# Sharing the homes of softmax buffers, and keeping an o weight piece by halves, in a recurrent attention with a gated FFN

## The chip, the cores and the metric

The kernel runs on one core of a Trainium2 chip. The metric is the device time of one execution in microseconds. A profile is one further execution; its span is counted from the first to the last instruction.

## The reference

A sequence of 2048 tokens with 1024 channels goes through two branches. Branch A is a recurrence over 64 segments of 32 tokens, with 32 heads of 128. Branch B is a feed-forward net of width 3584. A gate mixes the two.

```python
x = A_x
g = _sigmoid((x * gate_w).sum(-1, keepdims=True))
for s in range(n_seg):                       # branch A
    xs = x[:, s * seg_len:(s + 1) * seg_len, :].copy()
    h = jnp.concatenate([mem, xs], axis=1)   # 8 memory rows and 32 tokens
    q = jnp.einsum('btd,dhe->bhte', h, Wq)   # k and v in the same way
    ...
    scores = jnp.where(mask[None, None], scores, -1000000000.0)
    p = _softmax(scores, axis=-1)
    o = jnp.einsum('bhqk,bhke->bhqe', p, v)
    o = jnp.einsum('bhte,hed->btd', o, Wo)
    mem = o[:, :M, :].copy()                 # the next segment's memory
    outs.append(o[:, M:, :])
b = _gelu(x @ w_gate) * (x @ w_up) @ w_down  # branch B
return g * a + (1 - g) * b
```

All tensors are bf16. Each segment needs the memory rows that the segment before it has put out, so the 64 steps are a chain.

## The kernel before

**Stages.** Up to about 145 us the kernel transposes x, computes the gate and four of the 28 columns of the net's first layer, and loads the first attention weights. From there to about 1643 us it runs the 64 steps. Then comes branch B with the mix. An operation is recorded with `op(engine, function, rd=, wr=)`; a small planner turns reads and writes of 64-byte cells of SBUF, and of PSUM banks, into semaphore waits. Each engine runs its operations in program order. Two tiles at one address are therefore kept apart by waits alone.

**Weights.** Wq, Wk, Wv and Wo are 64 pieces of 128 x 2048 bf16, 512 KB each: letter, half u of the heads (0 or 1), number 0 to 7. They are more than SBUF holds beside the rest, which is room for 52 slots. In 40 slots one piece stays for good. In 12 a pair lives by turns: (k, 0, i) and (k, 1, i) for instance share a slot, and each step loads one of the two. `PAIRS` says which:

```python
PAIRS = {"k": (0, 2, 4), "q": (), "v": (0, 1, 2, 3, 4, 6), "o": (0, 1, 2)}
```

`proj(p, s)` multiplies with the piece at place p of the walk, then calls `spent(k)`, which has SyncE load the other piece of the pair into the slot (`fetch`, line 379). Odd steps take the halves in the other order, so that the piece loaded last is used first, without another load.

**One step.** `walk` gives 64 places: k and q of the first half by turns (16), v of the first half (8), k and q of the second half (16), then o of the first half and v of the second half interleaved, then o of the second half (8). Within the first half of a letter the paired pieces come first; within the second half they come last. A projection piece of q, k or v is four matmuls of 128x512 on four column groups of the array (lines 801 and 784); a piece of o is eight of 128x256 (line 812), four for each of its two heads.

**Fills.** The last 8 rows of each segment's tokens do not depend on the memory. Their q, k, v for four segments at once are computed by `fill` (line 831) and their output rows by `wo` (line 850), eight groups of matmuls each. They lie in between: three groups of `fa` ahead of the first attention, and in this version the other five behind the last v piece.

**Work hung into a step.** `on(letter, half, n, f)` puts work ahead of a place of the walk. In this order:
- `rest_k` (line 896) copies k of the last 8 tokens to columns 32 to 39 of kT, on POOL. It is called for the first head half early in a step, and for the second half after the first scores.
- `turn` transposes k and q and writes kT (ACT) and qT (DVE).
- `scores` (lines 713 to 727) writes a PSUM bank; it also has POOL clear pB.
- `softmax` (lines 730 to 743): exp to E8 on ACT; on DVE the sum, the reciprocal, the product pA, its transpose tA, the product pB, its transpose tB.
- `attend` (line 755) and `attend_tail` (line 767) multiply with tA and tB, then copy oT to SBUF on ACT and DVE, then oRc on POOL (line 778).

At the end of a step ACT writes a_bf (line 677), eight small transposing matmuls (line 1022) make the memory columns of the next hT, and the next step begins.

**DMA queues.** SyncE issues all weight loads, and those of qkr, hT and vB; ACT issues the stores; POOL issues oR and hR.

**Homes.** tA, E8, pA, pB each have a home of their own here; a_bf shares pA's, tB shares E8's.

Of the kernel before, what the change touches and what calls it, by code (L numbers as in the profile page):

```python
# [8 lines left out]
ALU = mybir.AluOpType  # L9
# [186 lines left out]
def bass_gated_mix__memory_aug_recurrent_mem_tr__geglu_ffn__prompt_kernel(  # L196
# [35 lines left out]
    with ExitStack() as es:  # L232
# [55 lines left out]
        oRc = al("oRc", [128, 2, NB, 16])  # L288
        vB = al("vB", [128, 2, 128])
        kT = al("kT", [128, 4, 4, LQ])  # L290
        tA = al("tA", [128, 8, 32])
        E8 = al("E8", [128, 8, LQ])
        oT = al("oT", [128, 4, 4, OW])
        tok = al("tok", [128, 512])
        stage = al("stg", [128, 512])
        pA = al("pA", [128, 8, 32])
        pB = al("pB", [128, 288])
        a_bf = al("a_bf", [128, 256], at=pA.off)
        vAs = [al("vA0", [128, 4, 128], at=oT.off), al("vA1", [128, 4, 128], at=tok.off)]
        qT = al("qT", [128, 4, 4, 32], at=stage.off)  # L300
        tok2 = al("tok2", [128, 512], at=oT.off + 1024)
        tB = al("tB", [128, 8, 32], at=E8.off)

        PIECE = 4096
        cur[0] = (cur[0] + 63) // 64 * 64
# [9 lines left out]
        NSLOT = NLOW + (top - cur[0]) // PIECE  # L315


        PAIRS = {"k": (0, 2, 4), "q": (), "v": (0, 1, 2, 3, 4, 6), "o": (0, 1, 2)}

        def seq(m, r):  # L320
            pairs = PAIRS[m] if m in "vo" else sorted({*PAIRS["k"], *PAIRS["q"]})
# [44 lines left out]
        def dst(t, k):  # L366
            return t[:, :].rearrange("p (h f) -> p h f", h=2) if k[0] == "o" else t[:, :]

        nlane = [0]
        done = [0] * len(hosts)  # L370

        def fetch(n):
            k, t = uses[n][done[n]], slots[n]
            if paired(k):
                lane = f"sl{n}"
            else:
                lane = f"res{nlane[0] % 8}"
                nlane[0] += 1
            op("sp", lambda e: e.dma_start(dst(t, k), src(k)), wr=[t.r()], lane=lane)  # L379

        def first(k):
            n = home[k]
            if done[n] == 0 and uses[n][0] == k:
                fetch(n)

        def spent(k):
# [41 lines left out]
        wgp = [al(f"wgp{h}", [128, KC, NJP * 64]) for h in range(2)]  # L428
        wup = [al(f"wup{h}", [128, KC, NJP * 64]) for h in range(2)]
        gpre = [al(f"gpre{i}", [128, NJP, FB]) for i in range(2)]  # L430
        memT = al("memT", [128, 64])
        xr1 = cur[0]
        cur[0] += 2 * TB * KC * 4 * NB
        assert cur[0] <= top
        cur[0] = low
        tp = [al(f"tp{t}", [128, FB], FP32) for t in range(2)]
        s1 = al("s1", [128, FB], FP32)
        xr = [al(f"xr{i}", [128, TB, KC, 4, NB], at=(cur[0], xr1)[i]) for i in range(2)]
        cur[0] += xr[0].nb
        tokB = al("tokB", [128, 512], at=oT.off)  # L440
        stv = al("stv", [128, 512], at=slots[-2].off)
        st0 = [al(f"st0{i}", [128, 4, 2, 128], at=slots[-1].off + 2048 * i) for i in range(2)]
        dl = al("dl", [128, NT], FP32, at=stage.off + stage.nb - 64)
        assert cur[0] <= dl.off
        hR1 = al("hR1", [128, KC, 32], at=pB.off)
        assert hR1.nb <= pB.nb
        hT = hTs[0]

        def gelu(hg, hu, bg, bu, n, gt, gt_r):
# [279 lines left out]
        def softmax():  # L729
            op("act", lambda e: e.activation(E8[:, :, :].rearrange("p a c -> p (a c)"), PB[SS][:, 0:320], ACTF.Exp, scale=scale),  # L730
               rd=[BK(SS)], wr=[E8.r()])
            op("dve", lambda e: e.tensor_reduce(sm, E8[:, :, :], AX.X, ALU.add), rd=[E8.r()], wr=[st8.r(8, 16)])
            op("dve", lambda e: e.reciprocal(sm, sm), rd=[st8.r(8, 16)], wr=[st8.r(8, 16)])
            op("dve", lambda e: e.tensor_tensor(out=pA[:, :, :], in0=E8[:, :, 0:32], in1=b8(sm, 32), op=ALU.mult),
               rd=[E8.r(), st8.r(8, 16)], wr=[pA.r()])
            op("dve", lambda e: e.transpose(tA[:, :, :].rearrange("p a c -> p (a c)"), pA[:, :, :].rearrange("p a c -> p (a c)")),
               rd=[pA.r()], wr=[tA.r()])
            op("dve", lambda e: e.tensor_tensor(
                out=pB[:, :].rearrange("p (j a) -> p j a", j=4)[:, :, 0:64].rearrange("p j (c k) -> p j c k", c=2)[:, :, :, 0:8],
                in0=E8[:, :, 32:40].rearrange("p (j c) k -> p j c k", c=2),  # L740
                in1=sm.rearrange("p (j c) -> p j c", c=2).unsqueeze(3).to_broadcast([128, 4, 2, 8]), op=ALU.mult),
               rd=[E8.r(), st8.r(8, 16)], wr=[pB.r()])
            op("dve", lambda e: e.transpose(tB[:, :, :].rearrange("p a c -> p (a c)"), pB[:, 0:256]),
               rd=[pB.r()], wr=[tB.r()])
# [13 lines left out]
                return ins  # L758
            op("pe", f, rd=[vA.r(), tA.r()], wr=[BK(b) for b in bo])

        def attend_tail(u, r):
            bo = bos[r]

            def f(e):
                for g in range(4):
                    r = slice(32 * g, 32 * g + 32)
                    ins = e.matmul(PB[bo[g]][:, 0:4 * OW].rearrange("p (j c) -> p j c", j=4)[:, :, NR:OW], lhsT=vB[r, u, :],  # L767
                                   rhs=tB[r, :, :].rearrange("p (j a) c -> p j (a c)", a=2)[:, :, NR:OW],
                                   start=False, stop=True, skip_group_check=True)
                return ins  # L770
            op("pe", f, rd=[tB.r(), vB.r()], wr=[BK(b) for b in bo])
            n = 4 * OW
# [16 lines left out]
        def proj(p, s):  # L789
            k = at_step(p, s)  # L790
            w = slots[home[k]]
            i = k[2]
            mine = spot[walk[p][:2]]
            one, end = p == mine[0], p == mine[-1]
            if k[0] != "o":
                h, bk = hTs[s % 2], bank_of[walk[p][:2]]

                def f(e):
                    for g in range(4):
                        at = PB[bk][32 * g:32 * g + 32, :], h[:, i, :], w[:, g * 512:(g + 1) * 512]  # L800
                        ins = again(e, g, *at, one, end) if k[0] == "q" else e.matmul(*at, start=one, stop=end)  # L801
                    return ins
                op("pe", f, rd=[h.r(32 * i, 32 * i + 32), w.r()], wr=[BK(bk)])
            else:
                r = walk[p][1]
                gp_, jj = i // 2, i % 2

                def f(e):
                    for hh in range(2):
                        for g in range(4):  # L810
                            c = hh * 1024 + g * 256
                            ins = e.matmul(PB[XO][32 * g:32 * g + 32, 0:256], lhsT=oT[:, gp_, 2 * jj + hh, 0:32],  # L812
                                           rhs=w[:, c:c + 256], start=(r == 0 and one and hh == 0), stop=(r == 1 and end and hh == 1))
                    return ins
                n = 4 * OW
                op("pe", f, rd=[oT.r(gp_ * n, (gp_ + 1) * n), w.r()], wr=[BK(XO)])
            spent(k)

        def holds(k, at_end=False):
# [20 lines left out]
        def wo(u, b, t=oR, ends=(True, True), at_end=False):  # L840
            out = []
            for n, i in enumerate([i for i in range(8) if i not in PAIRS["o"]] + list(PAIRS["o"])):
                k = ("o", u, i)
                w = (xo.get(k) if at_end else None) or slots[home[k]]

                def f(e, i=i, w=w, n=n):
                    for hh in range(2):
                        for g in range(4):
                            c = hh * 1024 + g * 256
                            ins = e.matmul(PB[b][32 * g:32 * g + 32, 0:256], lhsT=t[:, :, 2 * i + hh], rhs=w[:, c:c + 256],  # L850
                                           start=(ends[0] and n == 0 and hh == 0), stop=(ends[1] and n == 7 and hh == 1))
                    return ins

                def go(f=f, k=k, w=w):
                    holds(k, at_end)
                    op("pe", f, rd=[t.r(), w.r()], wr=[BK(b)])
                out.append(go)
            return out

# [43 lines left out]
        for s in range(NSEG):  # L903
# [12 lines left out]
            def on(m, r, n, *fs):  # L916
                at.setdefault(spot["k" if m == "q" else m, r][n], []).extend(fs)
# [6 lines left out]
            def some(fs, n=99):  # L924
                return lambda: run(fs, n)
# [46 lines left out]
            on("k", 1, 0, lambda: evac(bank_of["v", 0], vAs[0]))  # L972
            on("k", 1, 0, lambda: scores(ua))
            on("k", 1, 0, softmax)
            on("k", 1, 5, lambda: rest_k(ub))
            if uw is not None:
                on("k", 1, 5, lambda: load_oR(Q, uw))

# [1 line left out]
            on("o", 0, 0, lambda: evac(bank_of["q", 1], stage))  # L980
            on("o", 0, 0, some(fa, 3))
            on("o", 0, 0, lambda: attend(ua, 0))
            on("o", 0, 0, lambda: attend_tail(ua, 0))
            on("o", 0, 0, turn)
            on("o", 0, 3, lambda: scores(ub))
            on("o", 0, 3, softmax)

            on("o", 1, 0, lambda: evac(bank_of["v", 1], vAs[1]))
            on("o", 1, 0, some(fa))
            on("o", 1, 0, lambda: attend(ub, 1))  # L990
# [202 lines left out]
```

## Time and profile before

| | |
|---|---|
| three runs, median | 2194.36 us (2189.56 to 2199.25) |
| profiled execution | 2186.54 us, span 2184.8 us |
| mean granted TensorE clock | 0.985 |
| busy share | PE 91%, DVE 43%, ACT 30%, POOL 13% |
| moved by DMA | 528.78 MB, 490.16 MB of it read from HBM |
| weight loads in the steps | 394 of v, 205 of k, 205 of o, each 512 KB |
| stretch 145 to 1642 us | DMA share 0.85, 296 GB/s |

A row of a view names the line, the engine, the operation and out<-in; "sl" stands for all weight slots, so a load of v is "sl<-in_A_Wv_dram". PE's busy time counts matmuls that are in flight, so a high share does not say that PE has no time to spare. PEld is PE's loading of weights. In the chain of waits each row is a start, a length and what was running or moving then; "issue" is time without a wait that the profile shows. A load's "DMA to landing" is counted from the start of its issue to the last byte's semaphore.

### The profile page before, as it was taken

Reading aid. Unit: us, or ns where it says so; the run is one execution under the profiler, and the core shown is the slowest. Engines: PE = TensorE matmul, PEld = TensorE weight load, DVE = VectorE, ACT = ScalarE, POOL = GpSimd, SP = SyncE. Lnnn points to the kernel's source line nnn. Section 1 sums busy time; section 2 is a strip of 40 time slices with the busy share of each in tenths; the row PEclk is TensorE's granted clock in tenths of the full one; section 3 lists DMA queues with packets and bytes.
Section 4 is the critical chain, followed back from the end, with each engine's and each line's share of the span. In section 5 each row is a group of like instructions: output and inputs, shape, how many; then the busy total and the mean of one; then the engine's idle time right before and its main releaser. Section 6 shows DMA issues by size and latency. Waiting matters only on the chain.

```text
span 2184.8 us, 77490 instructions
## 1 busy us (share of the span) xinstructions
PE 1992.8 (91%) x38220; PEld 938.7 (43%) x32556; DVE 938.7 (43%) x2056; ACT 650.0 (30%) x1330; POOL 293.0 (13%) x589
## 2 busy tenths in 40 slices
PE   7878989989999898889899999999889999999999
PEld 4334444444444444444444444444344434243343
DVE  6433443444344344344434444443444526263462
ACT  4323333333333333333333333333322213032130
POOL 7211111111111111111111111111111000000000
PEclk9999999999999999999999999999998999999999
DMA  9988888888888888888878888888889200000000
GB/s 364 353 299 275 304 310 289 291 297 307 284 318 299 281 314 308 273 285 305 296 272 287 315 293 301 303 295 279 302 298 371 102 20 30 31 30 30 25 25 20
DMA packets 259022, 528.78 MB, mean 242 GB/s; under 512 B 56048, under 2 KB 109168, under 8 KB 258696
## 3 DMA queue, kind: packets, MB, share of 16 engines
q1 hardware_dynamic: 215968, 483.15, 62.2%
q10 hardware_dynamic: 34136, 20.19, 3.3%
q0 software_dynamic: 8592, 20.49, 2.6%
q8 instruction: 278, 4.55, 0.8%
q14 instruction: 48, 0.39, 0.1%
HBM read 490.16 MB, written 33.55 MB: 240 GB/s over the span
## 4 chain that ended last, share of the span: by engine, by line
PE 63%; DMA 31%; issue 2%; ACT 1%; DVE 1%; SPq 1%; POOL 0%; ACTq 0%; POOLq 0%; DVEq 0%
DMA sl<-in_A_Wv_dram 26%; PE pb L463 16%; PE pb L801 13%; PE pb L784 10%; PE pb L812 6%; PE pb L831 5%; PE pb L1148 4%; PE pb L691 3%; PE pb L850 3%; DMA sl<-in_A_Wo_dram 2%; PE pb L1126 1%; SPq L379 1%; DMA xr_scr<-xr 1%; ACT a_bf L677 1%; PE pb L755 1%
## 5 line engine op out<-in xcount | busy, mean ns | idle before, releaser
L801 PE MATMUL pb<-sl,hT 128*32 128x512 bf16 x8192 | 708.6, 381 | 98.3 <-DMA sl<-in_A_Wv_dram 83.7
L801 PEld LDWEIGHTS pb<-sl,hT 128*32 128x32 bf16 x8192 | 220.3, 96 | 496.7 <-issue 272.1
L784 PE MATMUL pb<-sl,hT 128*32 128x512 bf16 x4096 | 399.5, 379 | 0.0
L812 PE MATMUL pb<-sl,oT 128*32 128x256 bf16 x8192 | 287.0, 277 | 28.2 <-issue 21.3
L812 PEld LDWEIGHTS pb<-sl,oT 128*32 128x32 bf16 x8192 | 210.3, 98 | 72.1 <-issue 31.4
L831 PE MATMUL pb<-sl,hR 128*32 128x512 bf16 x3072 | 218.1, 394 | 19.6 <-DMA sl<-in_A_Wv_dram 10.7
L677 ACT ACTIVATE tok<-pb 128x512 bf16<-128x512 f32 x192 | 114.9, 598 | 300.2 <-PE pb L801 271.7
L778 POOL COPY oRc<-oT 128x128 bf16<-128x128 bf16 x128 | 96.9, 757 | 738.2 <-DVE oT L680 729.2
L463 PE MATMUL pb<-xT,wg 128*128 128x512 bf16 x768 | 183.1, 382 | 2.6 <-DMA wg<-in_B_w_gate_dram 2.6
L680 DVE CAST oT<-pb 128x256 bf16<-128x256 f32 x256 | 96.8, 420 | 203.9 <-PE pb L767 203.9
L463 PE MATMUL pb<-xT,wu 128*128 128x512 bf16 x768 | 182.5, 381 | 0.0
L451 ACT ACTIVATE s<-pb 128x512 f32<-128x512 f32 x112 | 66.9, 598 | 289.6 <-PE pb L463 289.6
L1148 PE MATMUL pb<-wd,GT 128*32 128x512 bf16 x1568 | 152.4, 379 | 0.0
L784 PE MATMUL pb<-wd,GT 128*32 128x512 bf16 x1568 | 152.4, 379 | 0.0
L677 ACT ACTIVATE vA<-pb 128x512 bf16<-128x512 f32 x128 | 76.4, 597 | 226.1 <-PE pb L801 226.1
L452 DVE SCALAR_TENSOR_TENSOR tp<-s,pb 128x512 f32<-128x512 f32 x112 | 76.8, 685 | 125.6 <-ACT s L451 125.2
L831 PEld LDWEIGHTS pb<-sl,hR 128*32 128x32 bf16 x3072 | 79.3, 98 | 103.9 <-issue 28.5
L726 DVE TENSOR_REDUCE st<-pb 128x8 f32<-128x320 f32 x128 | 63.0, 492 | 125.8 <-PE pb L720 125.7
L463 PEld LDWEIGHTS pb<-xT,wg 128*128 128x128 bf16 x768 | 75.1, 98 | 95.5 <-issue 6.6
L463 PEld LDWEIGHTS pb<-xT,wu 128*128 128x128 bf16 x768 | 75.5, 98 | 91.7 <-issue 1.9
L680 DVE CAST stg<-pb 128x512 bf16<-128x512 f32 x64 | 44.3, 692 | 155.2 <-PE pb L784 155.2
L455 DVE SCALAR_TENSOR_TENSOR tp<-tp,pb 128x512 f32<-128x512 f32 x112 | 77.0, 688 | 78.9 <-ACT tp L454 77.4
(107 smaller groups left out, 2046.2 us busy)
## 6 DMA issues: line engine op xcount, KB each, us to landing
sl<-in_A_Wv_dram SPq DMA_DIRECT2D x394, 512.0 KB, 8.8
sl<-in_A_Wk_dram SPq DMA_DIRECT2D x205, 512.0 KB, 5.9
sl<-in_A_Wo_dram SPq DMA_DIRECT2D x205, 512.0 KB, 7.7
sl<-in_A_Wq_dram SPq DMA_DIRECT2D x16, 512.0 KB, 13.3
qkr<-qk_scr SPq DMA_DIRECT2D x63, 128.0 KB, 8.2
qk_scr<-fqk ACTq DMA_DIRECT2D x29, 256.0 KB, 6.0
wd<-in_B_w_down_dram SPq DMA_DIRECT2D x7, 1024.0 KB, 15.3
xq_scr<-xTp SPq DMA_DIRECT2D x4, 1024.0 KB, 17.1
```

What stands on the lines that cost most here:

```text
L451: op("act", lambda e: e.activation(s1[:, :], hg, ACTF.Square, scale=SQ), rd=[BK(bg)], wr=[s1.r()])
L452: op("dve", lambda e: e.scalar_tensor_tensor(out=t[:, :], in0=s1[:, :], scalar=1.0, in1=hg, op0=ALU.add, op1=ALU.mult), rd=[BK(bg), s1.r() ...
L455: op("dve", lambda e: e.scalar_tensor_tensor(out=t[:, :], in0=t[:, :], scalar=1.0, in1=hu, op0=ALU.add, op1=ALU.mult), rd=[BK(bu), t.r()], ...
L463: ins = e.matmul(PB[bk][:, 0:FB], lhsT=w[:, kc, cc:cc + 128], rhs=x[:, :, :, kc, :].rearrange("p t i c -> p (t i) c"), start=(kc == 0), st ...
L677: op("act", lambda e: e.activation(o, i, ACTF.Copy), rd=rd, wr=wr)
L680: op("dve", lambda e: e.tensor_copy(o, i), rd=rd, wr=wr)
L778: op("pool", lambda e: e.tensor_copy(oRc[:, u, :, :].rearrange("p c (g j) -> p g j c", g=4), diag), rd=[oT.r()], wr=[oRc.r(128 * u, 128 * ...
L784: return e.add_instruction(mybir.InstMatmult(name=nc.get_next_instruction_name(), start_tensor_calc=start, stop_tensor_calc=stop, tile_siz ...
L801: ins = again(e, g, *at, one, end) if k[0] == "q" else e.matmul(*at, start=one, stop=end)
L812: ins = e.matmul(PB[XO][32 * g:32 * g + 32, 0:256], lhsT=oT[:, gp_, 2 * jj + hh, 0:32], rhs=w[:, c:c + 256], start=(r == 0 and one and hh ...
L831: ins = e.matmul(PB[b][32 * g:32 * g + 32, :], lhsT=h[:, k[2], :], rhs=w[:, g * 512:(g + 1) * 512], start=(n == 0), stop=(n == 7))
L1148: ins = again(e, q, *a, j == 0, j == NJ - 1) if hf else e.matmul(*a, start=(j == 0), stop=(j == NJ - 1))
```

## The change

1. **Pairs.** v has five pairs instead of six (3 leaves), o has four instead of three (3 joins). Slots stay 52.
2. **The o pair 3 by halves.** Its slot keeps the first head of both pieces for good. The second head, 256 KB, lives in a new tile `oh` of 2 KB per partition; each step loads the one of the other half into it.
3. **Homes.** E8 takes the home of qT (`stage`); pB and tB take that of kT; a_bf and hR1 that of tA; pA is gone, the product is made in place in E8, and the transpose reads E8 with a stride of 40 between blocks. At the start, xr and memT get other homes.
4. **Order.** rest_k of the second half comes behind the matmuls of the first attention instead of behind the first scores. Two groups of `fa` come ahead of the last five v pieces, so three instead of five stand behind the last.

```diff
+        tA = al("tA", [128, 8, 32])
+        oh = al("oh", [128, 1024])
+        a_bf = al("a_bf", [128, 256], at=tA.off)
+        E8 = al("E8", [128, 8, LQ], at=stage.off)
+        pB = al("pB", [128, 288], at=kT.off)
...
-        tB = al("tB", [128, 8, 32], at=E8.off)
+        tB = al("tB", [128, 8, 32], at=kT.off + 640)
...
-        PAIRS = {"k": (0, 2, 4), "q": (), "v": (0, 1, 2, 3, 4, 6), "o": (0, 1, 2)}
+        PAIRS = {"k": (0, 2, 4), "q": (), "v": (0, 1, 2, 4, 6), "o": (0, 1, 2, 3)}
+        HALF = 3
...
+        halved = lambda k: k[0] == "o" and k[2] == HALF
+
+        def heads_of(k):
+            t = slots[home[k]]
+            if not halved(k):
+                return [(t, 0), (t, 1024)]
+            return [(t, 1024 * k[1]), (oh, 0)]
...
         def fetch(n):
             k, t = uses[n][done[n]], slots[n]
+            if halved(k):
+                op("sp", lambda e: e.dma_start(oh[:, :], A_Wo[16 * k[1] + 2 * HALF + 1]), wr=[oh.r()], lane="oh")
+                return
...
-            op("dve", lambda e: e.tensor_tensor(out=pA[:, :, :], in0=E8[:, :, 0:32], in1=b8(sm, 32), op=ALU.mult),
-               rd=[E8.r(), st8.r(8, 16)], wr=[pA.r()])
-            op("dve", lambda e: e.transpose(tA[:, :, :].rearrange("p a c -> p (a c)"), pA[:, :, :].rearrange("p a c -> p (a c)")),
-               rd=[pA.r()], wr=[tA.r()])
+            op("dve", lambda e: e.tensor_tensor(out=E8[:, :, 0:32], in0=E8[:, :, 0:32], in1=b8(sm, 32), op=ALU.mult),
+               rd=[E8.r(), st8.r(8, 16)], wr=[E8.r()])
+            op("dve", lambda e: e.transpose(tA[:, :, :], E8[:, :, 0:32]),
+               rd=[E8.r()], wr=[tA.r()])
...
-            on("k", 1, 5, lambda: rest_k(ub))
...
-            on("o", 0, 0, lambda: attend_tail(ua, 0))
+            on("o", 0, 0, lambda: attend_tail(ua, 0, lambda: rest_k(ub)))
...
+            on("v", 1, 3, some(fa, 2))
```

After the last step, four o pieces of half 1 are loaded anew for the last `wo` instead of three.

More of the change, by code (lines that the diff above doesn't have):

```diff
@@ L290, in bass_gated_mix__memory_aug_recurrent_mem_tr__geglu_ffn__prompt_kernel @@
         kT = al("kT", [128, 4, 4, LQ])
-        tA = al("tA", [128, 8, 32])
-        E8 = al("E8", [128, 8, LQ])
         oT = al("oT", [128, 4, 4, OW])
@@ L295, in bass_gated_mix__memory_aug_recurrent_mem_tr__geglu_ffn__prompt_kernel @@
         stage = al("stg", [128, 512])
-        pA = al("pA", [128, 8, 32])
-        pB = al("pB", [128, 288])
-        a_bf = al("a_bf", [128, 256], at=pA.off)
+        tA = al("tA", [128, 8, 32])
[3 more added lines that the diff above has]
+        pB = al("pB", [128, 288], at=kT.off)
         vAs = [al("vA0", [128, 4, 128], at=oT.off), al("vA1", [128, 4, 128], at=tok.off)]
@@ L367, in dst, with regs @@
             return t[:, :].rearrange("p (h f) -> p h f", h=2) if k[0] == "o" else t[:, :]
+        halved = lambda k: k[0] == "o" and k[2] == HALF
[4 more added lines that the diff above has]
+            return [(t, 1024 * k[1]), (oh, 0)]
+        def regs(k):
+            return [t.r(c, c + 1024) for t, c in heads_of(k)]
         nlane = [0]
@@ L383, in first @@
             if done[n] == 0 and uses[n][0] == k:
+                if halved(k):
+                    t = slots[n]
+                    op("sp", lambda e: e.dma_start(t[:, :].rearrange("p (u f) -> p u f", u=2),
+                                                   A_Wo.rearrange("(u h) p f -> h p u f", u=2)[2 * HALF]), wr=[t.r()], lane="oh2")
                 fetch(n)
@@ L430, in bass_gated_mix__memory_aug_recurrent_mem_tr__geglu_ffn__prompt_kernel @@
         gpre = [al(f"gpre{i}", [128, NJP, FB]) for i in range(2)]
-        memT = al("memT", [128, 64])
+        memT = al("memT", [128, 64], at=oh.off)
         xr1 = cur[0]
-        cur[0] += 2 * TB * KC * 4 * NB
+        cur[0] += 4 * TB * KC * 4 * NB
         assert cur[0] <= top
@@ L437, in bass_gated_mix__memory_aug_recurrent_mem_tr__geglu_ffn__prompt_kernel @@
         s1 = al("s1", [128, FB], FP32)
-        xr = [al(f"xr{i}", [128, TB, KC, 4, NB], at=(cur[0], xr1)[i]) for i in range(2)]
-        cur[0] += xr[0].nb
+        xr = [al(f"xr{i}", [128, TB, KC, 4, NB], at=xr1 + i * 2 * TB * KC * 4 * NB) for i in range(2)]
         tokB = al("tokB", [128, 512], at=oT.off)
@@ L444, in bass_gated_mix__memory_aug_recurrent_mem_tr__geglu_ffn__prompt_kernel @@
         assert cur[0] <= dl.off
-        hR1 = al("hR1", [128, KC, 32], at=pB.off)
-        assert hR1.nb <= pB.nb
+        hR1 = al("hR1", [128, KC, 32], at=tA.off)
         hT = hTs[0]
@@ L759, in attend, with attend_tail @@
             op("pe", f, rd=[vA.r(), tA.r()], wr=[BK(b) for b in bo])
-        def attend_tail(u, r):
+        def attend_tail(u, r, then=None):
             bo = bos[r]
@@ L771, in attend_tail @@
             op("pe", f, rd=[tB.r(), vB.r()], wr=[BK(b) for b in bo])
+            if then:
+                then()
             n = 4 * OW
@@ L808, in f @@
                 def f(e):
-                    for hh in range(2):
+                    for hh, (w, c0) in enumerate(heads_of(k)):
                         for g in range(4):
-                            c = hh * 1024 + g * 256
+                            c = c0 + g * 256
                             ins = e.matmul(PB[XO][32 * g:32 * g + 32, 0:256], lhsT=oT[:, gp_, 2 * jj + hh, 0:32],
@@ L815, in proj @@
                 n = 4 * OW
-                op("pe", f, rd=[oT.r(gp_ * n, (gp_ + 1) * n), w.r()], wr=[BK(XO)])
+                op("pe", f, rd=[oT.r(gp_ * n, (gp_ + 1) * n)] + regs(k), wr=[BK(XO)])
             spent(k)
@@ L843, in wo, with f @@
                 k = ("o", u, i)
-                w = (xo.get(k) if at_end else None) or slots[home[k]]
-                def f(e, i=i, w=w, n=n):
-                    for hh in range(2):
+                w = xo.get(k) if at_end else None
+                ws = [(w, 0), (w, 1024)] if w else heads_of(k)
+                def f(e, i=i, ws=ws, n=n):
+                    for hh, (w, c0) in enumerate(ws):
                         for g in range(4):
-                            c = hh * 1024 + g * 256
+                            c = c0 + g * 256
                             ins = e.matmul(PB[b][32 * g:32 * g + 32, 0:256], lhsT=t[:, :, 2 * i + hh], rhs=w[:, c:c + 256],
@@ L852, in f, with go @@
                     return ins
-                def go(f=f, k=k, w=w):
+                def go(f=f, k=k, ws=ws):
                     holds(k, at_end)
-                    op("pe", f, rd=[t.r(), w.r()], wr=[BK(b)])
+                    op("pe", f, rd=[t.r()] + [w.r(c, c + 1024) for w, c in ws], wr=[BK(b)])
                 out.append(go)
```

## The prediction, made before the change had run

> **What bounds the kernel now.** I read the chain that ended last first, then the chain and the timelines inside one step of the recurrence, then the waits. Chain of the page, by engine and by line:
>
> ```profile
> PE 63%; DMA 31%; issue 2%; ACT 1%; DVE 1%; SPq 1%; POOL 0%; ACTq 0%; POOLq 0%; DVEq 0%
> DMA sl<-in_A_Wv_dram 26%; PE pb L463 16%; PE pb L801 13%; PE pb L784 10%; PE pb L812 6%; PE pb L831 5%; PE pb L1148 4%; PE pb L691 3%; PE pb L850 3%; DMA sl<-in_A_Wo_dram 2%; PE pb L1126 1%; SPq L379 1%; DMA xr_scr<-xr 1%; ACT a_bf L677 1%; PE pb L755 1%
> ```
>
> A quarter of the span is one transfer, the v weights, though PE is 91% busy on the page. Of the SyncE timeline of the step that starts at 899.7 us, the weight loads (start us, us of issuing):
>
> ```profile
> 899.67 2.38 SPq L379 DMA_DIRECT2D sl<-in_A_Wk_dram  x3
> 903.80 3.95 SPq L379 DMA_DIRECT2D sl<-in_A_Wv_dram  x6
> 912.97 1.41 SPq L379 DMA_DIRECT2D sl<-in_A_Wo_dram  x3
> ```
>
> The same step's chain of waits:
>
> ```profile
> 906.83 12.49 DMA sl<-in_A_Wv_dram
> 919.32 0.04 issue
> 919.36 0.40 PE pb L801 x4
> 919.76 1.08 PE pb L831 x20
> 920.84 0.23 PE pb L755 x16
> 921.07 0.07 PE pb L767 x4
> 921.14 1.03 PE pb L850 x32
> 922.17 1.79 PE pb L812 x64
> 923.96 0.02 issue
> 923.99 0.39 ACT a_bf L677
> ```
>
> The sixth v piece lands at 919.32. Behind it stand its projection (L801), five matmul groups of fills (L831), the attention, four groups of wo (L850), then the eight last o pieces (L812), 0.22 us each. The last of these starts at 922.00 + 7 x 0.22 = 923.54. The three o loads, from the load line's own view:
>
> ```profile
> L379 SPq DMA_DIRECT2D sl<-in_A_Wo_dram x3: 379/470/471, 913.0 to 913.9; - x3
> DMA to landing us min/median/max: 7.7/8.6/9.5
> ```
>
> They land at 913.0 + 7.7 = 920.7, then 922.0, then 913.9 + 9.5 = 923.4: in order, 1.35 us apart, straight behind the last v piece. So the last o piece arrives 0.15 us before PE wants it. **Two chains end almost together**: v landing plus PE's tail, and the landing of the last o piece. In all 63 steps after the first, read the same way, the o margin is under 0.3 us in 41 (median 0.22, mean 0.50). That the transfers themselves are full between 912 and 921 us shows here (DMA share, GB/s at the end):
>
> ```profile
> 912.00:915.00 3.00, 3.00 (x108) 2.57 (x108) 2.08 (x5) 1.16 (x4) 1.01 (x2) 1.00 1.03 419
> 915.00:918.00 3.00, 1.63 (x28) 0.43 (x20) 2.11 (x6) 0.43 (x1) 0.00 (x0) 1.00 1.02 406
> 918.00:921.00 3.00, 1.64 (x44) 0.75 (x44) 0.00 (x0) 0.60 (x1) 0.00 (x0) 1.00 1.02 372
> ```
>
> **What the Trainium skill says.** "DMA: Bandwidth & Descriptors", Queues, rings and completion order: on each DMA engine the descriptors of one ring are consumed in ring order. The trace agrees: v, then o, in issue order. Same page, Where 436 GB/s comes from: 16 ports give 435 GB/s; the trace has 406 to 419 with the engines full, so only fewer bytes help. "SBUF — State Buffer", The DMA setup-cost knee: a DMA pays about 2 us of fixed cost, mostly completion. Here pieces queued behind one another land every 1.35 us, so that cost is overlapped; no run here shows a 256 KB load in such a queue. "VectorE: DVE Perf Modes", The three transpose paths: it works on 32x32 blocks; what strides between the blocks cost is not on the page, nor in this trace.
>
> **The change part by part.** A piece of 512 KB takes 1.3 us (the spacing of back-to-back v pieces; 0.524 MB at 406 GB/s is 1.29).
>
> 1. One v pair less: per step five v loads instead of six. Last v landing: -1.30 us. The last v piece must find PE ready: in the last stretch PE waits about 2 us per step for v pieces (in the step shown 0.69 + 1.87 us and more), so yes in most steps.
>
> 2. A fourth o pair by halves: per step one load of 256 KB (oh) more, issued by SyncE after the u half's projection, at the next o place, about 0.7 us after the third o load's issue and some 7 us before its turn in the ring. Half a piece: +0.65 us. Last o landing: -1.30 + 0.65 = -0.65. What then waits for it is half a piece of matmuls (0.11) instead of a whole (0.22), another -0.11. The load of qkr moves behind it on SyncE's queue; who needs qkr, the POOL copy (L896, at 923.76 here), runs some 5 us before ACT next writes kT.
>
> 3. Two fills ahead of the last v pieces: five groups behind the last v piece become three, -0.43 us of PE. But the attention there also needs vA from ACT: in the five steps without fills it starts 1.25 us after the last v piece's matmul, with five fills 1.56. So -0.31. Steps that fill v have pieces 3, 5, 7 resident and no longer wait for a landing ahead of the first attention (10.7 us in all on the page's waits); that time falls into the DMA wait and counts nothing.
>
> 4. rest_k(ub), the POOL copy of 0.295 us, moves from behind the first scores to behind the first attention, because tB now lies in kT. Queued behind it on POOL: the oRc copy, which starts only after the oT copies; waiting for it: ACT's kT copy, then scores, the second softmax, the second attention. Timeline of before at that place:
>
> ```profile
> 911.78 0.25 PE L767 MATMUL pb<-tB,vB 32*128 32x160 bf16 x4
> 912.08 0.66 ACT L677 ACTIVATE oT<-pb 128x256 bf16<-128x256 f32 x2 [1.45 <-PE pb L767]
> 912.63 0.60 ACT L677 ACTIVATE kT<-pb 128x512 bf16<-128x512 bf16 x1
> ```
>
> ACT has two oT copies first, 0.6 to 0.69 us after the attention in nearly every step; POOL needs 0.07 (its answer to DVE at 912.91) + 0.295 = 0.37. Hidden by 0.25 us. It is also moved past the oR load on POOL's queue, in 30 steps; that issue ended 0.3 to 5 us before the attention in each. Cost 0, at most some tenths, which the second softmax's margin takes (tB is ready 0.7 us or more before PE's second attention in every step after the first, median 1.7).
>
> 5. The homes: E8 over qT, pB and tB over kT, the product in place, a_bf over tA. ACT's stage copy must now wait for DVE's last read of E8: it came 0.43 us after that or later. The memset of pB waits for the scores' end; DVE writes pB 3 us later. In-place product and strided transpose: 425 and 445 ns now; upper end 500 ns, the row of the 320-wide subtraction, lower end no change. Under the DMA wait: 0.
>
> 6. Outside the steps: 256 KB more at the start (0.65 us, in a stage with full DMA), one more xo load at the end, behind w1 whose matmuls take 17 us: taken as 0. The xr buffers move: 0, bounds -1 and +2 us.
>
> **Sum.** The v path gains 1.30 + 0.31 = 1.61 us a step where PE's waits allow it. The o path gains 0.65 + 0.11 + (margin - 0.04, the least margin seen). The step gains the smaller. With each step's own margin and waits: 41 steps with margin under 0.3 give 35.3 us (0.86 each), the other 22 give 27.4 (1.25 each); 62.8 together, minus 0.65 at the start: 62. Against the profile's span of 2184.8 that is 2.8%; the median of the runs, 2194.36, stands 0.4% above it, and taking 62 off it gives 2132.
>
> **The rivals.**
> A. As summed: 2132. Chance 0.60.
> B. The half load costs as much as a whole one (its fixed cost is not overlapped, or 2 KB rows slow it). Then the last o landing does not move, and a step gains 0.11 + margin - 0.04, capped by the v path: some 32 us, 2162. For it: nothing shows such a load. Against: o pieces, also in 2 KB rows, land as quickly as v pieces. 0.20.
> C. The o path doesn't bind, because its loads share the engines earlier than the landings suggest: then the v path decides everywhere, 93 us with PE's waits as cap, 2101. Against: 41 margins under 0.3. 0.08.
> D. Slower: rest_k held on POOL. It decides once it comes more than 0.25 + 1.7 = 2 us late, at the median. If the oR load, which waits for a transfer (up to 4.6 us on the page's waits), holds it 4 us behind the attention in its 30 steps, each loses 2 us, 60; the other 33 gain 32: 28 slower, 2222. Against: those issues ended before the attention. 0.08.
> E. A gain eaten by another wait (k pieces, PE's clock): about 2194. 0.04.
>
> **How the numbers follow.** About 0.5% (11 us) can be told from no change. Faster: A, B, C, 0.88; same 0.04; slower 0.08. The range takes in A with its unknowns, all of B with 8 us above it, and most of the way to C: 2105 to 2170.
>
> **What would show it.** v loads 394 to 331, oh loads 65 of 256 KB; PE's wait in the last stretch moves from Wv at L801 to Wo at L812, about 0.7 us a step; the chain shows "DMA oh" where "DMA sl<-in_A_Wv" stood; oh lands 0.65 us after the third o piece; L831 behind the last v piece is x12. Wrong, if PE still ends its waits on v, if oh lands 1.3 us behind, or if kT on ACT waits for POOL.

## The result, and the profile after

| | before | after |
|---|---|---|
| median of 4 runs, us | 2191.96 (2183.09 to 2199.25) | 2167.86 (2163.94 to 2170.37) |
| profiled span, us | 2184.8 | 2168.5 |

The ratio is 0.989, 95% interval 0.9849 to 0.9931: 24 us less, 1.1%. That lies in the range (2105 to 2170), but the forecast was 62 us. A second set of six runs gave 2170.58 us and 0.9885 (0.9837 to 0.9934).

The page of after, first its chain, by engine and by line:

```profile
PE 72%; DMA 20%; issue 4%; ACT 2%; DVE 1%; POOL 0%; SPq 0%; ACTq 0%; POOLq 0%; DVEq 0%
PE pb L820 17%; PE pb L480 16%; PE pb L803 13%; DMA oh<-in_A_Wo_dram 11%; PE pb L831 7%; DMA sl<-in_A_Wv_dram 4%; PE pb L708 4%; PE pb L1168 4%; PE pb L850 4%; PE pb L870 2%; DMA sl<-in_A_Wk_dram 1%; PE pb L1146 1%; PE pb L772 1%; DMA xr_scr<-xr 1%; ACT a_bf L694 1%
```

(Lines have moved: 801 is now 820, 812 is 831, 831 is 850, 850 is 870.) The v loads fell from 26% of the chain to 4%, and "DMA oh" stands there with 11%; PE grew from 63% to 72%, "issue" from 2% to 4%. The loads of the same page:

```profile
sl<-in_A_Wv_dram SPq DMA_DIRECT2D x331, 512.0 KB, 8.4
...
sl<-in_A_Wo_dram SPq DMA_DIRECT2D x204, 512.0 KB, 6.7
oh<-in_A_Wo_dram SPq DMA_DIRECT2D x65, 256.0 KB, 7.6
```

331 v loads and 65 half loads, as forecast. What PE waited for in the steps of after (141 to 1604 us; total, times, longest):

```profile
PE pb L831 <- issue: 47.8, 42, 2.7
PE pb L831 <- DMA sl<-in_A_Wo_dram: 14.4, 20, 1.7
PE pb L820 <- DMA sl<-in_A_Wv_dram: 14.2, 26, 1.4
PE pb L831 <- DMA oh<-in_A_Wo_dram: 5.4, 20, 1.4
```

And of before (141 to 1620 us):

```profile
PE pb L801 <- DMA sl<-in_A_Wv_dram: 81.6, 106, 1.9
PE pb L812 <- issue: 21.3, 27, 1.5
```

The wait for v is nearly gone (81.6 to 14.2 us), as forecast. A part came back as waits for o (14.4 and 5.4), another as "issue", in which PE stands still without a wait that the profile shows.

One step of after, the same step that the prediction shows of before; its first matmul is at 894.17 (before, 899.23). Its chain of waits:

```profile
908.17 7.26 DMA oh<-in_A_Wo_dram
915.43 0.04 issue
915.47 0.43 PE pb L831 x8
915.90 0.02 issue
915.93 0.39 ACT a_bf L694
```

The chain runs through the half load and then through all eight matmuls of its piece. In 37 of 62 steps PE starts this last piece 0.04 us after the landing, so it had waited for it; before, that was so in 12 steps. (The view of waits leaves out gaps under 0.15 us.) The loads on SyncE's timeline of that step:

```profile
906.61 1.41 SPq L394 DMA_DIRECT2D sl<-in_A_Wo_dram  x3
908.17 0.35 SPq L387 DMA_DIRECT2D oh<-in_A_Wo_dram  x1
```

The o loads go out 12.4 us after the step's first matmul; before, 912.97 - 899.23 = 13.7 in this step. On average it is 12.4 before and 12.3 after. The next table averages 62 steps (all but the first and last) of the traces of before and after, and of a second profile of after. A landing is the last byte's semaphore. Three names for what follows: the **lead** is the time from the first o issue to the last v landing, the **stretch** the time from the last v landing to the last o landing, the **tail** the time from the last landing to the next step's first matmul.

| mean of a step, us | before | after | again | forecast |
|---|---|---|---|---|
| last v landing, from the step's start | 17.62 | 16.40 | 16.32 | -1.30 |
| last v matmul to second attention | 1.53 | 1.15 | 1.15 | -0.31 |
| second attention, from the step's start | 19.24 | 17.88 | 17.78 | -1.61 |
| stretch | 4.19 | 5.26 | 5.23 | +0.65 |
| last o landing, from the step's start | 21.82 | 21.66 | 21.55 | -0.65 |
| tail | 1.97 | 1.92 | 1.81 | -0.35 |
| step | 23.79 | 23.58 | 23.35 | -1.00 |

The forecast of -0.35 is what the sum of 62.8 us over 63 steps leaves beside the landing: 0.11 for the half piece and 0.24 of margin. The table says where the gain went: the v side came near its forecast, the last o landing moved by a quarter (0.16) to two fifths (0.27) of what was forecast, and the tail shrank by 0.05 and 0.17. What follows the 62 steps is the same, 565 us.

### The profile page after: what moved, and what is told of

Same layout as the page of the kernel before. It is cut to its first block, busy times and chain, and to the rows that moved or that the text cites. A ratio compares the mean times of both kernels' runs of the same rounds, so it can differ in the third digit from the quotient of the medians.

```text
span 2168.5 us, 77621 instructions
## 1 busy us (share of the span) xinstructions
PE 1991.1 (92%) x38220; PEld 955.8 (44%) x32556; DVE 938.5 (43%) x2056; ACT 650.4 (30%) x1330; POOL 291.0 (13%) x589
## 4 chain that ended last, share of the span: by engine, by line
PE 72%; DMA 20%; issue 4%; ACT 2%; DVE 1%; POOL 0%; SPq 0%; ACTq 0%; POOLq 0%; DVEq 0%
PE pb L820 17%; PE pb L480 16%; PE pb L803 13%; DMA oh<-in_A_Wo_dram 11%; PE pb L831 7%; DMA sl<-in_A_Wv_dram 4%; PE pb L708 4%; PE pb L1168 4%; PE pb L850 4%; PE pb L870 2%; DMA sl<-in_A_Wk_dram 1%; PE pb L1146 1%; PE pb L772 1%; DMA xr_scr<-xr 1%; ACT a_bf L694 1%
## 5 line engine op out<-in xcount | busy, mean ns | idle before, releaser
L820 PE MATMUL pb<-sl,hT 128*32 128x512 bf16 x8192 | 714.8, 383 | 27.3 <-DMA sl<-in_A_Wv_dram 14.8
L820 PEld LDWEIGHTS pb<-sl,hT 128*32 128x32 bf16 x8192 | 234.3, 97 | 408.4 <-issue 275.1
L803 PE MATMUL pb<-sl,hT 128*32 128x512 bf16 x4096 | 407.5, 384 | 0.0
L831 PE MATMUL pb<-sl,oT 128*32 128x256 bf16 x7680 | 291.1, 274 | 71.9 <-issue 46.5
L831 PEld LDWEIGHTS pb<-sl,oT 128*32 128x32 bf16 x7680 | 204.7, 97 | 124.4 <-issue 80.5
L850 PE MATMUL pb<-sl,hR 128*32 128x512 bf16 x3072 | 225.9, 383 | 16.1 <-ACT stv L694 5.9
L697 DVE CAST hT<-pb 128x32 bf16<-128x32 f32 x63 | 12.1, 192 | 261.6 <-PE pb L1042 261.6
L850 PEld LDWEIGHTS pb<-sl,hR 128*32 128x32 bf16 x3072 | 85.7, 97 | 86.3 <-issue 30.3
```

Source lines behind the costliest of these rows:

```text
L697: op("dve", lambda e: e.tensor_copy(o, i), rd=rd, wr=wr)
L803: return e.add_instruction(mybir.InstMatmult(name=nc.get_next_instruction_name(), start_tensor_calc=start, stop_tensor_calc=stop, tile_siz ...
L850: ins = e.matmul(PB[b][32 * g:32 * g + 32, :], lhsT=h[:, k[2], :], rhs=w[:, g * 512:(g + 1) * 512], start=(n == 0), stop=(n == 7))
```

## The experiments

The theories in the expectations: **L**, the landing of the last o load ends the step, and what lengthens the stretch is what was lost. **S**, PE's own stalls ("issue") end it, and the landing would not matter. Within L: **A**, the o loads go out as late as before while the v loads end 1.3 us sooner, so their turn comes before they are ready to move; **C**, other queues' transfers, which used to lie behind the landing, now share the stretch. Ratios are to the kernel before, with 95% intervals; landing, stretch, tail and step are means, as in the table.

**1. No half load** (leaves out the reloading of oh, so the second head of o piece 3 is stale).

```diff
-                op("sp", lambda e: e.dma_start(oh[:, :], ...
+                if done[n] == 0:
+                    op("sp", lambda e: e.dma_start(oh[:, :], ...
```

> The changed kernel without its load of oh in the steps: the second heads of o piece 3 are loaded once at the start and never again, so the output is computed with stale weights there; all matmuls stay. Theory L (the landing of the last o load ends the step): the third o load becomes the last to land, 0.77 us earlier in the mean step; where PE's own chain does not bind first, the step shortens by 0.4 to 0.77 us, 25 to 45 us less than the changed kernel's 2168, so 2123 to 2143. Theory S (PE's own stalls and arithmetic end the step since the v wait shrank): under 10 us less, 2158 to 2168.

2144.79 us, 0.978 (0.9733 to 0.9827): 23 us below after. Last landing 20.83 instead of 21.66, step 23.09 instead of 23.58. This is just short of what L expected and more than twice the most that S allowed. L is right, but the step gained only 0.49 of the landing's 0.83 us, since PE's own work is close behind the landing.

**2. Another 256 KB ahead of the half load.**

```diff
+                if done[n]:
+                    op("sp", lambda e: e.dma_start(t[:, c:c + 1024], ...), lane="oh2")
                 op("sp", lambda e: e.dma_start(oh[:, :], ...
```

> The changed kernel with another 256 KB per step in front of oh: the first head of o piece 3 of the half just used is loaded again over itself. Theory L: oh lands 0.7 us later in each step and the step ends as much later wherever oh was awaited (its margin was at the least value in more than half of the steps): 30 to 45 us more than the changed kernel, 2198 to 2213. Theory S: PE has reserve in front of oh, under 10 us more, 2168 to 2178.

2204.41 us, 1.0054 (1.0034 to 1.0074): 37 us above after; last landing 22.38, step 24.09. The two halves land 1.46 us behind the third o piece, the one half of after 0.77. L again, and a half load costs half a piece.

**3. Piece 3 as two operations**, so that only its last four matmuls wait for oh.

```diff
-                op("pe", f, rd=[...] + regs(k), wr=[BK(XO)])
+                for hs in ((0,), (1,)) if halved(k) else ((0, 1),):
+                    op("pe", lambda e, hs=hs: f(e, hs), rd=[...] + [regs(k)[h] for h in hs], wr=[BK(XO)])
```

> The changed kernel with o piece 3 as two operations, so that only the four matmuls of its second head wait for oh; before, all eight did. In the trace of the changed kernel the piece's fifth matmul starts 0.19 us after oh has landed at the least, so all eight stand behind it. Theory L: 0.11 us less in each step that waits for oh: 4 to 7 us less than the changed kernel, 2161 to 2164. Theory S: no change.

2160.73 us, 0.9851 (0.9815 to 0.9888). A second set of runs:

> The kernel with piece 3 as two operations once more, to see whether it is faster than the kernel after by itself: after the median of the kernel after in two sets of runs (2168 and 2171), 2158 to 2164 if the four matmuls taken from behind the half load are worth the 0.11 us a step, 7 us, of the forecast; 2166 to 2171 if they are not.

2163.11 us, 0.9856 (0.9815 to 0.9897). What the edit acts on is seen on PE's timeline of after at 915 us:

```profile
915.47 0.29 PE L831 MATMUL pb<-sl,oT 128*32 128x256 bf16 x4 [0.20 <-DMA oh<-in_A_Wo_dram]
915.59 0.28 PE L831 MATMUL pb<-oh,oT 128*32 128x256 bf16 x4
```

The four matmuls that read the slot, which has held its weights for good, wait for oh too. In the kernel with two operations, the chain of waits ends a step so:

```profile
950.37 8.38 DMA oh<-in_A_Wo_dram
958.75 0.04 issue
958.79 0.32 PE pb L831 x4
```

Four instead of eight, 0.11 us less. The tail shows it where the landing ends the step: in the shortest quarter of the steps it is at most 1.32 us in both sets, and 1.43 in both profiles of after. Its mean does not (1.82 and 1.88, after 1.92 and 1.81), since other stalls move it more. Only 34 and 31 of 62 steps wait for oh with these last four matmuls, so the 0.11 us accounts for some 4 us. The medians are 7 us (0.3 to 0.4%) below after's, but the intervals overlap: a gain is likely, its size is not settled.

**4. Without the two fills ahead.**

```diff
-            on("v", 1, 3, some(fa, 2))
```

> The changed kernel without the two fill groups ahead of the last v pieces: five stand behind the last v piece again. Theory L: the second attention comes 0.31 to 0.43 us later, but PE waited about 0.9 us per step for o pieces after it, so the end of the step hardly moves: 0 to 6 us more than the changed kernel, 2168 to 2174. Theory S (PE's chain behind the last v ends the step): 0.3 to 0.4 us per step, 20 to 26 us more, 2188 to 2194.

2165.76 us, 0.9878 (0.9829 to 0.9928): no change. The v side lost 0.33 us (last v matmul to attention 1.48 instead of 1.15), and the time shows nothing of it: the last o landing comes at 21.64.

**5. The fills alone, in the kernel before.**

```diff
+            on("v", 1, 3, some(fa, 2))
```

> The kernel before with one part of the change: two fill groups ahead of the last v pieces. Theory L (two chains, the third o landing with a margin of 0.22 us at the median): the second attention comes 0.31 us earlier, but the last o piece then waits; the step gains its margin less 0.04, at most 0.31: 8 to 14 us less than before, 2178 to 2184. If PE's chain alone ended the step: 18 to 20 us less, 2172.

2184.32 us, 0.997 (0.9951 to 0.9989), 7 us less: there the last v landing still leads in part of the steps. Last v matmul to attention is 1.24 instead of 1.53, but the last o matmuls then wait (from the second half's first o matmul to its last 2.19 us instead of 1.90).

**6. The homes alone, in the kernel before**: shared homes, product in place, rest_k behind the attention, xr moved; the pairs and the fills stay as they were.

> The kernel before with the homes of the change, the product in place, the later rest_k and the moved xr buffers, without the other pairs, the half piece or the earlier fills. As priced in the prediction the steps do not move (0, at most 0.1 us a step); the steps begin about 3 us earlier if the moved xr buffers are why they do in the changed kernel (141.5 against 144.7 us): 2186 to 2192. If rest_k or the shared homes cost what eats the gain: 20 us or more above before.

2191.53 us, 1.0005 (0.9981 to 1.0028). These parts cost nothing that shows. The two instructions in that kernel's profile:

```profile
L733 DVE STREAM_TRANSPOSE tA<-E 128x256 bf16<-128x256 bf16 x128 | 57.0, 445 | 4.4
L731 DVE TENSOR_TENSOR E<-E,st 128x256 bf16<-128x256 bf16 x128 | 54.4, 425 | 4.4
```

445 and 425 ns, the durations of before.

**7. The three fills ahead of the first attention moved behind it**, so that the o loads go out earlier (A).

```diff
-            on("o", 0, 0, some(fa, 3))
-            on("v", 1, 3, some(fa, 2))
+            on("v", 1, 3, some(fa, 5))
```

> The changed kernel with the three fill groups that stood ahead of the first attention moved to the two ahead of the last v pieces, so five there. PE reaches the first o pieces, and SyncE issues the o loads, up to 0.65 us earlier; nothing is left out. Theory A (the o loads stretch because they are issued only 4.0 us ahead of the last v landing where it was 5.3, so that the queue behind v is not filled in time): the four o loads take 0.15 to 0.2 us less from the last v landing to the last byte, and the step ends as much earlier: 8 to 14 us less than the changed kernel, 2154 to 2160. Theory C (they stretch because stores and small loads of the end of the step now fall into them): no change, 2166 to 2170.

2162.99 us, 0.9865 (0.9833 to 0.9898). It did not do what it was made for. The first attention came 0.67 us earlier, the first o load at 12.21 us of the step instead of 12.34, and the second profile of after has 12.21 too: SyncE issues that load when the first o piece is done on PE, and that piece hardly moved. Part of the reason is a wait that the fills had covered, here and in after:

```profile
PE pb L708 <- ACT stg L694: 22.0, 63, 0.7
PE pb L708 <- ACT stg L694: 1.2, 4, 0.3
```

The lead is 4.25 us instead of 4.05, the stretch 5.15 instead of 5.26 (5.23): too little to tell A from C. Together with the two operations:

> The kernel after with both edits that came out a little faster alone: piece 3 as two operations, of which only the second waits for the half load, and the three fills ahead of the first attention moved behind it. If the two act on different things (matmuls behind the last landing; the issue of the o loads), their gains of 5 to 8 us each add up: 10 to 16 us faster than the kernel after, 2152 to 2158 beside a kernel before of 2192. If both only shift the same stalls of PE, the gain is that of one, 5 to 8 us. Theory A says in addition: lead above 4.2 us, last v landing to last o landing at most 5.15.

2162.81 us, 0.9852 (0.9813 to 0.9891): no better than the two operations alone. The sum of two gains is not there.

**8. The o loads later, in the kernel before, by their place in the program.**

```diff
+                if p == spot["v", 1][1]:
+                    while hold:
+                        fetch(hold.pop(0))
```

> The kernel before with one thing changed: the three o loads of a step are issued behind the second v piece of the second half, 1.6 us later. Theory A (the changed kernel's o loads stretch because they are issued with 4.0 instead of 5.3 us of lead before the last v landing): with 3.7 us of lead the stretch from the last v landing to the last o landing grows from 4.19 to about 4.5 us; each step ends 0.2 to 0.3 us later: 12 to 19 us more than before, 2203 to 2210. Theory C (stores and small loads): no change, 2188 to 2195.

2191.97 us, 0.9994 (0.9969 to 1.0018). A miss: SyncE does not run in step with PE, and what holds the load is the release of its slot, so it went out when it had before (at 12.32 us of the step instead of 12.37; lead 5.35). It tells nothing of A.

**9. The same with a real wait.**

```diff
-                        fetch(hold.pop(0))
+                        fetch(hold.pop(0), [last_v[0]])
```

> The kernel before, with its three o loads made to wait for the second v piece's matmuls of the second half, so that they are really issued later; nothing else is moved and no byte is added. The o loads should go out some 1.4 us later, the time from the first o issue to the last v landing falls from 5.2 to about 3.8 us. Theory A (the o loads are issued too close to their turn in the queue): the time from the last v landing to the last o landing grows from 4.19 to 4.5 to 4.7 us, and the run is 12 to 25 us slower than the kernel before. Theory C (other transfers in that stretch take the time): it stays at 4.2, and the run is within 5 us of the kernel before.

2234.28 us, 1.0182 (1.0132 to 1.0231); no byte more than before. The first o load went out 2.05 us later, the lead fell from 5.26 to 3.20 us (further than intended), the stretch grew from 4.19 to 5.02, the last landing from 21.82 to 22.64, the step by 0.72; the last v landing stayed (17.62). What PE waits for in the steps:

```profile
PE pb L808 <- DMA sl<-in_A_Wv_dram: 83.0, 109, 1.8
PE pb L821 <- DMA sl<-in_A_Wo_dram: 37.5, 53, 1.7
```

A wait for o that the kernel before hardly had (1.5 us in all). A is a real mechanism. The steps sorted by their lead, with the mean stretch (number of steps); after is less its own half load:

| lead, us | under 3 | 3 to 3.6 | 3.6 to 4.2 | 4.2 to 5 | over 5 |
|---|---|---|---|---|---|
| o loads later (9) | 5.61 (23) | 4.85 (28) | 4.37 (4) | 4.20 (6) | 3.94 (1) |
| before | | 5.42 (1) | 4.70 (1) | 4.24 (18) | 4.13 (42) |
| after | 5.68 (3) | 4.75 (10) | 4.37 (28) | 4.39 (15) | 4.26 (6) |

The last v landing is the end of the lead and the start of the stretch, so within one kernel a late landing alone lengthens the one and shortens the other: the rows do not prove A. The comparison of the means does, because only the issue was moved.

**10. The stores later** (C).

```diff
-            on("o", 1, 4, o_store)
-                on("o", 1, 0, lambda: store_v(k2[1], G, tok))
-            pend = [(0, [a_store])]
+            pend = [(0, [a_store, o_store])]
+                pend.append((0, [lambda u=k2[1], G=G: store_v(u, G, tok)]))
```

> The changed kernel with the o store and the v store of each step put at the beginning of the next step, where the transfers are nearly idle. Theory C: the DMA engines' time of the store queue between the last v landing and the last o landing, 0.20 us a step, goes away, and the step ends 0.15 to 0.2 us earlier: 9 to 13 us less than the changed kernel, 2155 to 2159. Theory A: under 4 us.

2392.04 us, 1.0902 (1.086 to 1.0945). A miss, by a wait that the edit itself makes (waits of ACT):

```profile
ACT tok L694 <- DMA v_scr<-tok: 289.6, 30, 12.9
```

The next step's tok has to wait for the v store, 9.7 us each time. With the o store alone moved:

> The changed kernel with the o store alone put at the beginning of the next step (the run that moved both stores made ACT wait for the v store, since the next step needs its tile). Theory C: half of the store queue's time between the last v and the last o landing goes away, 0.1 us a step: 4 to 8 us less than the changed kernel. Theory A: under 3 us.

2179.82 us, 0.9936 (0.9916 to 0.9957). The stretch shrank by 0.1 us (5.15), as C says, but the next step's v loads then came later (first v landing 11.01 instead of 10.45 us, last 16.84 instead of 16.40): moving this store costs more than it brings. The other transfers in the stretch were not moved, so this sets no bound on C.

**11. Fewer weight loads on PE** (leaves out 120 of its weight loads in each step, so those matmuls use a stale stationary operand). It tests whether PE's stalls come from its instructions.

> The changed kernel with 120 weight loads of PE per step left out (of some 955 PE instructions): the second head of every o piece and most v pieces multiply with the weights that the array still holds, so the output is computed with wrong stationary operands there; the matmuls, their number, shapes and data from SBUF and all transfers but PE's own instructions stay. Theory I (PE's stalls that the profile calls issue, 80 us in 68 gaps over 0.55 us in the steps of the changed kernel, are its instructions arriving late: they end 1.4 us after a 16 KB transfer of the instruction queue): 13% fewer instructions, the instruction transfers drop from 278 to about 248, stalls fall by half or more, 20 to 40 us less than the changed kernel, 2128 to 2148. Rival W (the stalls have another cause, and weight loads are hidden under matmuls): no change, within 5 us.

2176.99 us, 0.9933 (0.9904 to 0.9962): 6 us above after in the same set (12), where theory I expected 20 to 40 below. Waits of PE in the steps:

```profile
PE pb L833 <- DMA sl<-in_A_Wo_dram: 40.5, 55, 2.0
PE pb L803 <- DMA sl<-in_A_Wv_dram: 38.2, 54, 2.2
PE pb L833 <- DMA oh<-in_A_Wo_dram: 9.3, 43, 0.3
PE pb L734 <- issue: 7.8, 6, 2.3
PE pb L833 <- issue: 5.0, 6, 2.2
```

and the queue that brings the instructions, in its page:

```profile
q8 instruction: 248, 4.06, 0.7%
```

It was 278 transfers of 16 KB before and after. The stalls at the o matmuls (L831, here L833) fell from 47.8 us, and 32.9 in the second profile, to 5.0. So they go with PE's instructions; whether with their number or with the weight loads themselves, this run can't tell. The tail shrank from 1.92 to 1.54 us, but the landings came 0.50 us later (last o 22.16; from the second v piece on), and waits for loads took the place of the stalls. Why the landings came later isn't settled.

**12. After once more**, beside these: 2170.58 us, 0.9885, in the table above.

> The changed kernel itself once more, as the reference on the chip that runs the others: 2160 to 2172, 0.985 to 0.992 of before.

## Why the prediction was partly right, and where it failed

**Right.** Both paths were read rightly: the last v landing moved by -1.23 (again -1.31; forecast -1.30), the step from there to the attention by -0.38 (forecast -0.31), and the bound moved to the landing of the half load (experiments 1 and 2), so rival C is out. PE took only 0.98 us of the 1.23, because in 26 of 62 steps the last v piece now lies ready before PE comes to it (2 before), and its waits for v were 1.40 us a step before, not "about 2 us". This cost nothing, as the v path still ended first. Homes, product in place, strided transpose and rest_k cost nothing that shows (6), so rival D is out. The start cost nothing that shows either: the steps begin at 141.5 and 143.6 us, before 144.7.

**Rival B is out too, though its 2162 is nearer.** It said that a half load costs a whole piece. It lands 0.77 us behind the third o piece (median 0.71; forecast 0.65), a whole one 1.37 to 1.52 behind the one ahead. The Trainium skill, "SBUF — State Buffer", The DMA setup-cost knee, gives about 2 us of fixed cost for a DMA; behind the third o piece it does not show, since 0.77 is little more than half of a whole piece's time.

**The step that failed first** is "Last o landing: -1.30 + 0.65 = -0.65". It took the stretch as fixed but for the half load. The stretch grew by 1.07 us instead of 0.65, and the landing moved by -0.16 and -0.27 in the two profiles. Of the 0.42 too much, 0.12 is the half load (0.77). Most of the rest fits A: "some 7 us before its turn in the ring" was counted from before, but the first o load is issued when PE is done with the first o piece (12.32 us of the step before, 12.30 after), while the v pieces ahead of it landed 1.23 us sooner. The lead fell from 5.26 to 4.05 us (4.11). Putting each of after's 62 steps at the stretch that experiment 9 shows for its lead gives (3 x 1.42 + 10 x 0.66 + 28 x 0.18) / 62 = 0.26 us more than before. This is an estimate: few of that kernel's steps have the leads of after.

The packets of the traces give the same from another side. The window is the stretch, set back by the 0.55 us from a load's last packet to its semaphore. Weight loads move 1044 KB in it before and 1398 after (again 1393). Of the 354 KB more, 256 are the half load; the other 98 had been moved ahead of the last v landing before. At the 44 ns per KB of one engine that the packets show, spread over 16 engines, they are 0.27 us. The two counts agree. C is at work too: all other packets take 0.79 us of the 16 engines' time in the window before and 1.05 after. But the engines stand idle 0.21 us less in the window, which pays for most of it.

**The second** is "half a piece of matmuls (0.11) instead of a whole (0.22), another -0.11". The piece is one operation with one wait, and all eight matmuls stood behind it. The diff showed this: the tile oh is in the read list of the whole operation. Measured 0: the shortest tail is 1.43 us before and after, and 1.32 with two operations (3).

**The third** is the margin, 0.24 us a step. PE's last piece starts 0.49 us behind the landing before and 0.35 after (again 0.26), 0.04 at least in each: 0.14 and 0.23 came. But from there to the next step it takes 1.58 and 1.55 us instead of 1.48. The median is 1.41 to 1.42 in all three profiles; the slowest tenth of the steps takes over 2.01 and 1.87 instead of 1.64. All rows of PE's waits with "issue" together are 38.5 us before (47 times) and 78.4 and 67.8 after (80 and 85), from 141 to 1640 us. That such stalls mostly fell into the wait for v before, and stand by themselves now that it is gone, is the likely reading; no run shows it by itself. Rival E ("another wait") named this only in general; PE's granted clock, its other example, was no lower (0.985 before, 0.989 after). Experiment 11 shows that with fewer of these stalls PE follows the landing more closely, but also that the time is then lost in the landings, so the stalls and the loads lie close to each other and neither is the bound alone.

Together, per step: forecast 0.65 + 0.11 + 0.24 = 1.00; measured 0.16 and 0.27 from the landing, 0 from the half piece, 0.14 and 0.23 from the margin, less 0.09 and 0.07 behind the last piece: 0.21 and 0.44. Over 62 steps this is 13 and 27 us, on both sides of the 24 that the runs show.

**Open:** why the landings come later with fewer PE instructions, what each stall of PE waits for, and how exactly the growth of the stretch divides between A and C, since what C costs net of the idle time was not tested by itself.

## What to carry to other kernels

When loads are taken out ahead of others in a queue, the later ones gain only as far as they are issued early enough for their new turn: look at what sets their issue, and keep the lead (here 5.3 us before and 4.1 after). Here a wait belongs to an operation and not to an operand: split the operation if only part of it needs what comes last. Time that PE spends waiting for a load may also hide its other stalls, so count on getting back less than the wait.

## What the runs showed that was not expected

- Stalls of PE marked "issue" of over 0.55 us end 1.40 us (median; quartiles 1.34 to 1.47) after the end of a 16 KB transfer of the instruction queue in after; at random times this would be 3.1 (1.6 to 5.1). With experiment 11 this speaks for instructions that arrive late; it isn't shown directly.
- In after, packets of 2 KB took 150, 96 and 91 ns on average in the three microseconds from 13 to 16 us of the step, where the o loads begin; before they begin at 14 us, with 92 and 85. The median is 84 in all.
- Moving a load in the program order did not move its issue (8), and a wait for a PE operation that delayed it by 2.05 us cost 1.8% (9).
